# Squeeze-and-excitation gate on one core: keeping 16 rows in PSUM and three more in SBUF between two passes over the input

## Chip, cores and metric

One core of a Trainium2 chip. The time is device microseconds of that core, the median of several executions. "GB/s" is what the core's 16 DMA engines moved.

## The reference, cut to what matters

```python
x: (1, 256, 256, 384) bf16        # 65,536 positions, 384 channels, 50.3 MB
w_down: (384, 24), w_up: (24, 384)

def reference(x, w_down, w_up):
    s = x.mean(axis=(1, 2))
    s = sigmoid(silu(s @ w_down) @ w_up)
    return x * s[:, None, None, :]
```

Every output needs the mean over all positions. So the kernel passes over `x` twice: once to sum it, once to scale it. What is still on the chip after the first pass need not be read again.

## The kernel before

The positions are laid out as 128 partitions of 512 rows; a row is 384 bf16, 768 bytes in each partition, 98,304 bytes in all. Chunks of 16 rows (1.57 MB) go into 17 slots of SBUF. There are 32 chunks: 17 stay in the slots after the first pass ("cached"), 15 do not ("streamed") and are read again.

```python
JS = min(J, max(1, 12288 // (C * 2)))           # 16 rows in a chunk
n_slots = max(1, min(NCH, (avail - small_bytes) // bytes_per_slot))   # 17
NS = NCH - n_slots                               # 15 streamed chunks
p1_order = [(stream_ids[k], k % n_slots) for k in range(NS)] + [
    (cache_ids[i], i) for i in range(n_slots)]
# ... first pass: DMA a chunk (the last one in 8 pieces of 2 rows, the one before in 2),
#     then one matmul with a column of ones per row, all into one PSUM accumulator
nc.sync.dma_start(out=st[:, r0:r0 + rsz, :], in_=x3[:, j0 + r0:j0 + r0 + rsz, :])
nc.tensor.matmul(sums_ps[ci][:1, :csz], ones_bf[:, 0:1], st[:, jj, c0:c0 + csz], start=first, stop=last)
# ... mean, the two small products, sigmoids -> gate [128, 384] bf16
# second pass:
def scale_and_store(sl, ch, piece_rows=None):   # ... cut
    nc.vector.tensor_tensor(out=st[:, r0:r0 + rsz, :], in0=st[:, r0:r0 + rsz, :], in1=gate_b, op=ALU.mult)
    nc.scalar.dma_start(out=out3[:, j0 + r0:j0 + r0 + rsz, :], in_=st[:, r0:r0 + rsz, :])

for i in range(n_slots):        # cached chunks; slot 0 in pieces of 1, 3, 4, 8 rows, slot 1 in 8, 8
    ...
for k in range(NS):             # streamed chunks: read again into slot k, scale, store
    nc.sync.dma_start(out=slots[sl][:, :jsz, :], in_=x3[:, j0:j0 + jsz, :])
    scale_and_store(sl, stream_ids[k])
```

Of the kernel before, what the change touches and what calls it, by code (L numbers as in the profile page):

```python
# [8 lines left out]
ALU = mybir.AluOpType  # L9
ACT = mybir.ActivationFunctionType  # L10
BF16 = mybir.dt.bfloat16
FP32 = mybir.dt.float32


def _pad32(nbytes: int) -> int:
    return ((nbytes + 31) // 32) * 32
# [3 lines left out]
def kernel(  # L20
# [7 lines left out]
    nc = tc.nc  # L28
    P = nc.NUM_PARTITIONS

    B, H, W, C = x.shape
    Cd, R = w_down.shape
# [3 lines left out]
    J = N // P  # L36

    ck_chunks = [(c0, min(128, C - c0)) for c0 in range(0, C, 128)]
    KT = len(ck_chunks)
    cn_chunks = [(c0, min(512, C - c0)) for c0 in range(0, C, 512)]  # L40

    JS = min(J, max(1, 12288 // (C * 2)))
    chunks = [(j0, min(JS, J - j0)) for j0 in range(0, J, JS)]
    NCH = len(chunks)

    bytes_per_slot = _pad32(JS * C * 2)
    small_bytes = (
        _pad32(C * 2)
        + _pad32(8 * 2)
        + _pad32(KT * R * 2)  # L50
        + _pad32(C * 2)
        + _pad32(C * 2)
        + _pad32(KT * 2)
        + _pad32(4)
        + _pad32(P * 2)
        + _pad32(4)
    )
    avail = nc.sbuf_top - nc.sbuf_base
    n_slots = max(1, min(NCH, (avail - small_bytes) // bytes_per_slot))

    NS = NCH - n_slots
    stream_ids = list(range(NS))
    cache_ids = list(range(NS, NCH))

    x3 = x.flatten_outer_dims().rearrange("(p j) c -> p j c", p=P)
    out3 = out.flatten_outer_dims().rearrange("(p j) c -> p j c", p=P)

    slots_pool = ctx.enter_context(tc.tile_pool(name="slots", bufs=1))
    consts = ctx.enter_context(tc.tile_pool(name="consts", bufs=1))
    work = ctx.enter_context(tc.tile_pool(name="work", bufs=1))  # L70
    psum = ctx.enter_context(tc.tile_pool(name="psum", bufs=1, space=bass.MemoryType.PSUM))

    slots = [
        slots_pool.tile([P, JS, C], BF16, name=f"slot{i}") for i in range(n_slots)
    ]

    ones_bf = consts.tile([P, 8], BF16)
# [5 lines left out]
    sums_ps = [  # L83
        psum.tile([1, csz], FP32, name=f"sums_ps_{i}")
        for i, (c0, csz) in enumerate(cn_chunks)
    ]

    p1_order = [(stream_ids[k], k % n_slots) for k in range(NS)] + [
        (cache_ids[i], i) for i in range(n_slots)
    ]  # L90
    total_mm = J
    mm_state = {"idx": 0}

    def read_and_reduce(ch, sl, pieces):
        j0, jsz = chunks[ch]
        st = slots[sl]
        cuts = []
        step = (jsz + pieces - 1) // pieces
        r = 0
        while r < jsz:  # L100
            cuts.append((r, min(step, jsz - r)))
            r += step
        for (r0, rsz) in cuts:
            nc.sync.dma_start(  # L104
                out=st[:, r0:r0 + rsz, :], in_=x3[:, j0 + r0:j0 + r0 + rsz, :]
            )
            for jj in range(r0, r0 + rsz):
                first = mm_state["idx"] == 0
                last = mm_state["idx"] == total_mm - 1
                for ci, (c0, csz) in enumerate(cn_chunks):  # L110
                    nc.tensor.matmul(  # L111
                        sums_ps[ci][:1, :csz],
                        ones_bf[:, 0:1],
                        st[:, jj, c0:c0 + csz],
                        start=first,
                        stop=last,
                    )
                mm_state["idx"] += 1

    for n, (ch, sl) in enumerate(p1_order):  # L120
        remaining = len(p1_order) - n
        if remaining == 1:
            pieces = 8
        elif remaining == 2:
            pieces = 2
        else:
            pieces = 1
        read_and_reduce(ch, sl, pieces)

    wd_sb = consts.tile([P, KT, R], BF16)  # L130
    for kt, (c0, csz) in enumerate(ck_chunks):
        nc.gpsimd.dma_start(out=wd_sb[:csz, kt, :], in_=w_down[c0:c0 + csz, :])  # L132
    wu_sb = consts.tile([R, C], BF16)
    nc.gpsimd.dma_start(out=wu_sb[:R, :], in_=w_up[:, :])  # L134

    mean_bf = work.tile([1, C], BF16)
    for ci, (c0, csz) in enumerate(cn_chunks):
        nc.vector.tensor_scalar(  # L138
            out=mean_bf[:1, c0:c0 + csz],
            in0=sums_ps[ci][:1, :csz],  # L140
            scalar1=1.0 / float(N),
            scalar2=None,
            op0=ALU.mult,
        )

    meanT_ps = psum.tile([P, KT], FP32)
    for kt, (c0, csz) in enumerate(ck_chunks):
        nc.tensor.matmul(  # L148
            meanT_ps[:csz, kt:kt + 1],
            mean_bf[0:1, c0:c0 + csz],  # L150
            ones_bf[0:1, 0:1],
            start=True,
            stop=True,
        )
# [3 lines left out]
    else:  # L158
        for kt, (c0, csz) in enumerate(ck_chunks):
            nc.vector.tensor_copy(  # L160
                out=meanT_sb[:csz, kt:kt + 1], in_=meanT_ps[:csz, kt:kt + 1]
            )

    z1_ps = psum.tile([R, 1], FP32)
    for kt, (c0, csz) in enumerate(ck_chunks):
        nc.tensor.matmul(  # L166
            z1_ps[:R, 0:1],
# [2 lines left out]
            start=(kt == 0),  # L170
            stop=(kt == KT - 1),
# [5 lines left out]
        out=z1bc[:R, :],  # L177
        in0=z1_ps[:R, 0:1].to_broadcast([R, P]),
# [2 lines left out]
        op0=ALU.mult,  # L181
    )

    gate = consts.tile([P, C], BF16)
    for ci, (c0, csz) in enumerate(cn_chunks):
        zz_ps = psum.tile([P, csz], FP32, name=f"zz_ps_{ci}")
        nc.tensor.matmul(  # L187
            zz_ps[:, :csz],
            z1bc[:R, :],
            wu_sb[:R, c0:c0 + csz],  # L190
            start=True,
            stop=True,
        )
        nc.scalar.activation(  # L194
            out=gate[:, c0:c0 + csz], in_=zz_ps[:, :csz], func=ACT.Sigmoid
        )

    def scale_and_store(sl, ch, piece_rows=None):
        j0, jsz = chunks[ch]
        st = slots[sl]  # L200
        if piece_rows is None:
            cuts = [(0, jsz)]
        else:
            cuts = []
            r = 0
            for pr in piece_rows:
                if r >= jsz:
                    break
                pr = min(pr, jsz - r)
                cuts.append((r, pr))  # L210
                r += pr
            if r < jsz:
                cuts.append((r, jsz - r))
        for (r0, rsz) in cuts:
            gate_b = gate[:, None, :].to_broadcast([P, rsz, C])
            nc.vector.tensor_tensor(  # L216
                out=st[:, r0:r0 + rsz, :],
                in0=st[:, r0:r0 + rsz, :],
                in1=gate_b,
                op=ALU.mult,  # L220
            )
            nc.scalar.dma_start(
                out=out3[:, j0 + r0:j0 + r0 + rsz, :], in_=st[:, r0:r0 + rsz, :]
            )

    for i in range(n_slots):
        if i == 0:
            scale_and_store(i, cache_ids[i], piece_rows=[1, 3, 4, 8])
        elif i == 1:
            scale_and_store(i, cache_ids[i], piece_rows=[8, 8])  # L230
        else:
            scale_and_store(i, cache_ids[i])
    for k in range(NS):
        sl = k % n_slots
        j0, jsz = chunks[stream_ids[k]]
        nc.sync.dma_start(out=slots[sl][:, :jsz, :], in_=x3[:, j0:j0 + jsz, :])  # L236
        scale_and_store(sl, stream_ids[k])


# [28 lines left out]
```

## Time and profile before

| | before |
|---|---|
| time, median (12 runs, 306.75 to 307.49) | 307.19 us |
| span of the profiled run | 305.5 us |
| moved by the DMA: read, written | 73.96 MB, 50.33 MB |
| rows read twice | 240 of 512 |
| sum ready, first scale starts | 123.94 us, 126.75 us |
| last scale ends | 253.0 us |

The engines are named as the profiler names them: PE is TensorE, DVE is VectorE, ACT is ScalarE, POOL is GpSimd, SP is SyncE. These lines are from the page of the kernel before: its span, then the busy tenths of DVE and of the DMA engines and the GB/s in 40 equal slices of the span, then two DMA queues (packets, MB, share of the 16 engines) and the HBM total.

```profile
span 305.5 us, 1315 instructions
...
DVE  0000000000000000599999999998444441000000
...
DMA  7999999999999999299999999999999999999996
GB/s 295 420 426 429 423 426 426 425 423 428 425 424 428 425 422 351 74 351 380 436 428 425 434 436 418 434 434 426 426 434 428 428 431 436 425 428 436 426 425 288
...
q1 hardware_dynamic: 7920, 73.93, 57.9%
q10 hardware_dynamic: 5184, 50.33, 39.0%
...
HBM read 73.96 MB, written 50.33 MB: 407 GB/s over the span
```

The DMA engines are 90% or more busy in nearly every slice, and most slices move 418 to 436 GB/s. The hole in slice 17 is the gate: the last input has landed, and nothing can be written yet. DVE is idle for the last six slices, while the DMA works on to the end: the writes have queued up behind it.

The same kernel in chosen stretches. The columns are: stretch, length, busy time (and count) of PE, PE weight loads, DVE, ACT and POOL, then the granted clock, the DMA share and GB/s. A share above 1 comes from counting a packet where it starts.

```profile
core 0: us, PE busy (x) PEld busy (x) DVE busy (x) ACT busy (x) POOL busy (x), PEclk, DMA share, GB/s
24.00:100.00 76.00, 57.44 (x325) 27.44 (x323) 0.00 (x0) 0.00 (x0) 0.00 (x0) 0.98 1.01 425
117.00:121.00 4.00, 4.00 (x27) 2.04 (x25) 0.00 (x0) 0.00 (x0) 0.00 (x0) 1.00 1.05 376
134.00:144.00 10.00, 0.00 (x0) 0.00 (x0) 10.00 (x4) 0.00 (x0) 0.00 (x0) 0.50 1.03 372
150.00:240.00 90.00, 0.00 (x0) 0.00 (x0) 75.53 (x23) 0.00 (x0) 0.00 (x0) 0.50 1.01 430
250.00:295.00 45.00, 0.00 (x0) 0.00 (x0) 2.99 (x1) 0.00 (x0) 0.00 (x0) 0.50 1.01 430
```

Reading alone gets 425 GB/s, mixed reads and writes 430, writes alone 430. So bytes can be turned into time: a row read or not read in the mixed stretch is 98,304 bytes / 430 GB/s = 0.229 us. The Trainium skill, "DMA: Bandwidth & Descriptors" (Where 436 GB/s comes from), puts the ceiling of the SBUF ports at 435 GB/s. This trace stays just under it, at 425 to 430. Two stretches are below that rate. From 117 to 121 us, where the 2-row pieces move (with the end of the two 8-row pieces before them), it is 376. From 134 to 144 us it is 372.

The timeline around the gate (start, length, engine, line, operation, output and inputs, count, and in brackets how long the engine was idle before and for what) and the last scale.

```profile
start us, us, engine line op out<-in xcount [idle before <-releaser]
...
115.48 8.43 PE L111 MATMUL sums_ps<-slot,ones_bf 128*1 128x384 bf16 x48 [0.93 <-DMA slot<-in_x_dram]
...
123.94 0.55 DVE L138 TENSOR_SCALAR mean_bf<-sums_ps 1x384 bf16<-1x384 f32 x1 [123.07 <-PE sums_ps L111]
...
126.75 1.90 DVE L216 TENSOR_TENSOR slot<-slot,gate 128x384 bf16<-128x384 bf16 x3 [0.95 <-ACT gate L194]
```

```profile
249.63 3.36 DVE L216 TENSOR_TENSOR slot<-slot,gate 128x6144 bf16<-128x6144 bf16 x1 [3.98 <-DMA slot<-in_x_dram]
```

The last full chunk lands at about 115.5 us; PE then does the 48 rows that are left in one go, 8.4 us, and DVE turns the sum into the mean at 123.94. The first scale starts at 126.75. The last scale ends at 249.63 + 3.36 = 253.0 us, 50 us before the last write lands.

### The profile page before, as it was taken

What the parts mean: (1) busy time and instruction counts of PE and PEld (TensorE: products, weight loads), DVE (VectorE), ACT (ScalarE), POOL (GpSimd) and SP (SyncE); (2) the same over time, 40 slices, a digit from 0 to 9 for tenths busy, and PEclk for the clock granted to TensorE, in tenths of its full rate; (3) what the DMA queues carried; (4) which work ended last, traced back from release to release, by engine and by line L of the source; (5) the groups of instructions that cost most, each with busy time, mean ns of one, the idle gap of its engine ahead of it and who ended that gap; (6) DMA issues with size and microseconds to landing.
All of it is one profiled execution on the core that took longest, in us unless ns stands there. A gap on an engine that the chain in (4) does not pass through costs nothing.

```text
span 305.5 us, 1315 instructions
## 1 busy us (share of the span) xinstructions
PE 92.7 (30%) x519; PEld 44.3 (14%) x519; DVE 106.6 (35%) x40; ACT 2.1 (1%) x4; POOL 2.5 (1%) x8
## 2 busy tenths in 40 slices
PE   0977787777777778300000000000000000000000
PEld 0433333333333334100000000000000000000000
DVE  0000000000000000599999999998444441000000
ACT  1000000000000000000000000000000000000000
POOL 3000000000000000000000000000000000000000
PEclk9999899999999999855555555555555555555555
DMA  7999999999999999299999999999999999999996
GB/s 295 420 426 429 423 426 426 425 423 428 425 424 428 425 422 351 74 351 380 436 428 425 434 436 418 434 434 426 426 434 428 428 431 436 425 428 436 426 425 288
DMA packets 13238, 124.38 MB, mean 407 GB/s; under 512 B 1572, under 2 KB 2736, under 8 KB 3632
## 3 DMA queue, kind: packets, MB, share of 16 engines
q1 hardware_dynamic: 7920, 73.93, 57.9%
q10 hardware_dynamic: 5184, 50.33, 39.0%
q8 instruction: 4, 0.07, 0.1%
q0 software_dynamic: 128, 0.04, 0.1%
q14 instruction: 2, 0.02, 0.0%
HBM read 73.96 MB, written 50.33 MB: 407 GB/s over the span
## 4 chain that ended last, share of the span: by engine, by line
DMA 57%; DVE 21%; PE 3%; SPq 1%; issue 0%; ACT 0%
DMA slot<-in_x_dram 45%; DVE slot L216 20%; DMA out_dram<-slot 12%; PE sums_ps L111 3%; SPq L104 1%; DVE mean_bf L138 0%; ACT gate L194 0%; DVE z1bc L176 0%; PE zz_ps L187 0%; PE meanT_ps L148 0%; PE z_ps L166 0%; DVE meanT_sb L157 0%; ACT s L174 0%; SPq L236 0%
## 5 line engine op out<-in xcount | busy, mean ns | idle before, releaser
L216 DVE TENSOR_TENSOR slot<-slot,gate 128x6144 bf16<-128x6144 bf16 (+4 forms) x36 | 105.5, 2995 | 21.7 <-DMA slot<-in_x_dram 20.7
L111 PE MATMUL sums_ps<-slot,ones_bf 128*1 128x384 bf16 x512 | 91.9, 335 | 32.0 <-DMA slot<-in_x_dram 32.0
L111 PEld LDWEIGHTS <-ones_bf 128*1 128x1 bf16 x512 | 43.8, 86 | 79.7 <-issue 42.8
L138 DVE TENSOR_SCALAR mean_bf<-sums_ps 1x384 bf16<-1x384 f32 x1 | 0.5, 545 | 123.1 <-PE sums_ps L111 123.1
L132 POOL DMA_DIRECT2D wd_sb<-in_w_down_dram x3 | 1.8, 605 | 0.8 <-POOLq L252 0.8
L81 ACT ACT_TABLE_LOAD x1 | 1.3, 1283 | 0.7 <-PEq L252 0.7
L174 ACT ACTIVATE s<-z_ps 24x1 f32<-24x1 f32 x1 | 0.2, 160 | 123.0 <-PE z_ps L166 123.0
L134 POOL DMA_DIRECT2D wu_sb<-in_w_up_dram x1 | 0.5, 539 | 0.0
L187 PE MATMUL zz_ps<-wu_sb,z1bc 24*128 24x384 bf16 x1 | 0.3, 331 | 0.6 <-DVE z1bc L176 0.6
L176 DVE TENSOR_SCALAR z1bc<-z_ps,s 24x128 bf16<-24x128 f32 x1 | 0.3, 339 | 0.5 <-ACT s L174 0.5
L194 ACT ACTIVATE gate<-zz_ps 128x384 bf16<-128x384 f32 x1 | 0.5, 491 | 0.8 <-PE zz_ps L187 0.8
L148 PE MATMUL meanT_ps<-ones_bf,mean_bf 1*128 1x1 bf16 x3 | 0.2, 163 | 0.6 <-DVE mean_bf L138 0.6
L78 DVE MEMSET ones_bf<- 128x8 bf16 x1 | 0.1, 65 | 0.8 <-PEq L252 0.8
L166 PE MATMUL z_ps<-meanT_sb,wd_sb 128*24 128x1 bf16 x3 | 0.2, 163 | 0.3 <-DVE meanT_sb L157 0.3
L148 PEld LDWEIGHTS <-mean_bf 1*128 1x128 bf16 x3 | 0.1, 92 | 1.0 <-DVE mean_bf L138 1.0
L157 DVE CAST meanT_sb<-meanT_ps 128x3 bf16<-128x3 f32 x1 | 0.2, 165 | 0.3 <-PE meanT_ps L148 0.3
L166 PEld LDWEIGHTS <-wd_sb 128*24 128x24 bf16 x3 | 0.2, 90 | 0.3 <-issue 0.2
L81 ACT ACTIVATE dummy<-ones_bf 1x1 f32<-1x1 bf16 x1 | 0.2, 202 | 0.0
L187 PEld LDWEIGHTS <-z1bc 24*128 24x128 bf16 x1 | 0.1, 90 | 0.7 <-DVE z1bc L176 0.7
L252 POOL MEMSET const-bfloat16-1.0<- 128x1 bf16 x1 | 0.1, 102 | 0.0
L252 POOL MEMSET const-float32-0.0<- 128x1 f32 x1 | 0.1, 100 | 0.2 <-issue 0.2
L252 POOL MEMSET const-float32-1.0<- 128x1 f32 x1 | 0.1, 100 | 0.0
(1 smaller groups left out, 0.1 us busy)
## 6 DMA issues: line engine op xcount, KB each, us to landing
slot<-in_x_dram SPq DMA_DIRECT2D x45, 1536.0 KB, 29.4
out_dram<-slot ACTq DMA_DIRECT2D x30, 1536.0 KB, 29.2
out_dram<-slot ACTq DMA_DIRECT2D x3, 768.0 KB, 3.7
slot<-in_x_dram SPq DMA_DIRECT2D x2, 768.0 KB, 26.8
slot<-in_x_dram SPq DMA_DIRECT2D x8, 192.0 KB, 11.7
out_dram<-slot ACTq DMA_DIRECT2D x1, 384.0 KB, 2.4
out_dram<-slot ACTq DMA_DIRECT2D x1, 288.0 KB, 2.1
out_dram<-slot ACTq DMA_DIRECT2D x1, 96.0 KB, 1.7
```

What stands on the lines that cost most here:

```text
L81: nc.scalar.activation(out=dummy[:1, :1], in_=ones_bf[0:1, 0:1], func=ACT.Sigmoid)
L104: nc.sync.dma_start(out=st[:, r0:r0 + rsz, :], in_=x3[:, j0 + r0:j0 + r0 + rsz, :])
L111: nc.tensor.matmul(sums_ps[ci][:1, :csz], ones_bf[:, 0:1], st[:, jj, c0:c0 + csz], start=first, stop=last,)
L132: nc.gpsimd.dma_start(out=wd_sb[:csz, kt, :], in_=w_down[c0:c0 + csz, :])
L134: nc.gpsimd.dma_start(out=wu_sb[:R, :], in_=w_up[:, :])
L138: nc.vector.tensor_scalar(out=mean_bf[:1, c0:c0 + csz], in0=sums_ps[ci][:1, :csz], scalar1=1.0 / float(N), scalar2=None, op0=ALU.mult,)
L148: nc.tensor.matmul(meanT_ps[:csz, kt:kt + 1], mean_bf[0:1, c0:c0 + csz], ones_bf[0:1, 0:1], start=True, stop=True,)
L166: nc.tensor.matmul(z1_ps[:R, 0:1], wd_sb[:csz, kt, :], meanT_sb[:csz, kt:kt + 1], start=(kt == 0), stop=(kt == KT - 1),)
L187: nc.tensor.matmul(zz_ps[:, :csz], z1bc[:R, :], wu_sb[:R, c0:c0 + csz], start=True, stop=True,)
L194: nc.scalar.activation(out=gate[:, c0:c0 + csz], in_=zz_ps[:, :csz], func=ACT.Sigmoid)
L216: nc.vector.tensor_tensor(out=st[:, r0:r0 + rsz, :], in0=st[:, r0:r0 + rsz, :], in1=gate_b, op=ALU.mult,)
L252: nc = _bacc.Bacc("TRN2", target_bir_lowering=False, num_devices=1)
```

## The change

Intent: read fewer rows twice. PSUM has room that the kernel does not use. The new kernel copies the first chunk into six PSUM banks (parts of PSUM; one holds 1,024 bf16 in each partition) during the first pass and scales it from there at the very end. It also saves small tiles: `mean` and `gate` are laid over `w_up`'s tile. With that the last slot holds 19 rows instead of 16. Rows read twice: 512 - 16 (PSUM) - (17 x 16 + 3) (slots) = 221 instead of 240. They are one chunk of 13 rows, now first in order, and 13 chunks of 16.

The Trainium skill, "PSUM — Partial Sum Buffer" (Specifications (TRN2)), lists no DMA access to PSUM, and for VectorE only writes of 4-byte types. That is why the rows go through a slot and DVE on the way in and on the way out, and why the copy in is done on pairs of bf16 seen as fp32.

The diff, cut to its core:

```diff
+    n_slots = max(1, min((J + JS - 1) // JS, (avail - bytes_small) // slot_bytes))      # 17
+    spare = avail - bytes_small - n_slots * slot_bytes
+    extra_rows = max(0, min(spare // _pad32(C * 2), max(0, J - n_slots * JS)))          # 3
+    PR = JS  # rows kept in PSUM
+    streamed_rows = J - cached_rows - PR
+    rem = streamed_rows % JS
+    if rem:
+        stream_chunks.append((j0, rem))        # 13 rows, first
+        j0 += rem
 ...
+    pbanks = [psum.tile([P, 512], FP32, name=f"pbank{b}") for b in range(NB)]           # 6
+    misc_ps = psum.tile([P, 512], FP32, name="misc_ps")      # all small results of the gate
 ...
+    LAST = [6, 5, 4, 2, 2]                     # pieces of the last slot; before: 8 of 2 rows
+    read_and_reduce(0, PR, 14)                 # first chunk, through slot 14
+    flat0 = slots[14].rearrange("p r c -> p (r c)")
+    for b in range(NB):
+        nc.vector.tensor_copy(out=pbanks[b][:, :],
+            in_=flat0[:, b * 1024:(b + 1) * 1024].bitcast(FP32))
 ...
-    gate = consts.tile([P, C], BF16)
+    gate = wu_mean                             # w_up, the mean and the gate share a tile
 ...  (after the last streamed chunk)
+    e = 0
+    while e < PR * C:                          # 14 pieces: whole rows, and parts of rows
+        ...                                    #   where a bank ends inside a row
+        nc.vector.tensor_tensor(out=dst, in0=src, in1=g, op=ALU.mult)     # PSUM -> slot 14
+        e += n
+    nc.scalar.dma_start(out=out3[:, 0:PR, :], in_=slots[14][:, :PR, :])
```

More of the change, by code (lines that the diff above doesn't have):

```diff
@@ L42 @@
     JS = min(J, max(1, 12288 // (C * 2)))
-    chunks = [(j0, min(JS, J - j0)) for j0 in range(0, J, JS)]
-    NCH = len(chunks)
-    bytes_per_slot = _pad32(JS * C * 2)
-    small_bytes = (
-        _pad32(C * 2)
-        + _pad32(8 * 2)
+    MP = 32 if R <= 32 else 0
+    bytes_small = (
+        _pad32(8 * 2)
         + _pad32(KT * R * 2)
         + _pad32(C * 2)
-        + _pad32(C * 2)
+        + (_pad32(C * 2) if MP == 0 else 0)
         + _pad32(KT * 2)
@@ L58 @@
     avail = nc.sbuf_top - nc.sbuf_base
-    n_slots = max(1, min(NCH, (avail - small_bytes) // bytes_per_slot))
-    NS = NCH - n_slots
-    stream_ids = list(range(NS))
-    cache_ids = list(range(NS, NCH))
+    slot_bytes = _pad32(JS * C * 2)
+    n_slots = max(1, min((J + JS - 1) // JS, (avail - bytes_small) // slot_bytes))
+    spare = avail - bytes_small - n_slots * slot_bytes
+    extra_rows = max(0, min(spare // _pad32(C * 2), max(0, J - n_slots * JS)))
+    slot_rows = [JS] * n_slots
+    slot_rows[-1] = JS + extra_rows if J > n_slots * JS else min(JS, J - (n_slots - 1) * JS)
+    cached_rows = min(J, sum(slot_rows))
+    PR = JS
+    streamed_rows = J - cached_rows - PR
+    stream_chunks = []
+    j0 = PR
+    rem = streamed_rows % JS
+    if rem:
+        stream_chunks.append((j0, rem))
+        j0 += rem
+    while j0 < PR + streamed_rows:
+        stream_chunks.append((j0, JS))
+        j0 += JS
+    NS = len(stream_chunks)
+    cache_chunks = []
+    j0 = PR + streamed_rows
+    for i in range(n_slots):
+        rows = min(slot_rows[i], J - j0)
+        if rows <= 0:
+            break
+        cache_chunks.append((j0, rows))
+        j0 += rows
+    assert j0 == J
+    n_slots = len(cache_chunks)
     x3 = x.flatten_outer_dims().rearrange("(p j) c -> p j c", p=P)
@@ L73 @@
     slots = [
-        slots_pool.tile([P, JS, C], BF16, name=f"slot{i}") for i in range(n_slots)
+        slots_pool.tile([P, slot_rows[i], C], BF16, name=f"slot{i}")
+        for i in range(n_slots)
     ]
@@ L86, with reduce_rows, read_and_reduce @@
     ]
-    p1_order = [(stream_ids[k], k % n_slots) for k in range(NS)] + [
-        (cache_ids[i], i) for i in range(n_slots)
-    ]
+    NB = PR * C // 1024
+    pbanks = [psum.tile([P, 512], FP32, name=f"pbank{b}") for b in range(NB)]
+    misc_ps = psum.tile([P, 512], FP32, name="misc_ps")
     total_mm = J
     mm_state = {"idx": 0}
-    def read_and_reduce(ch, sl, pieces):
-        j0, jsz = chunks[ch]
+    def reduce_rows(st, r0, rsz):
+        for jj in range(r0, r0 + rsz):
+            first = mm_state["idx"] == 0
+            last = mm_state["idx"] == total_mm - 1
+            for ci, (c0, csz) in enumerate(cn_chunks):
+                nc.tensor.matmul(
+                    sums_ps[ci][:1, :csz],
+                    ones_bf[:, 0:1],
+                    st[:, jj, c0:c0 + csz],
+                    start=first,
+                    stop=last,
+                )
+            mm_state["idx"] += 1
+    def read_and_reduce(j0, jsz, sl, pieces=1):
         st = slots[sl]
@@ L99, in read_and_reduce @@
         r = 0
-        while r < jsz:
-            cuts.append((r, min(step, jsz - r)))
-            r += step
+        for n in LAST if pieces == 4 else [step] * pieces:
+            cuts.append((r, n))
+            r += n
+        assert r == jsz
         for (r0, rsz) in cuts:
@@ L106, in read_and_reduce @@
             )
-            for jj in range(r0, r0 + rsz):
-                first = mm_state["idx"] == 0
-                last = mm_state["idx"] == total_mm - 1
-                for ci, (c0, csz) in enumerate(cn_chunks):
-                    nc.tensor.matmul(
-                        sums_ps[ci][:1, :csz],
-                        ones_bf[:, 0:1],
-                        st[:, jj, c0:c0 + csz],
-                        start=first,
-                        stop=last,
-                    )
-                mm_state["idx"] += 1
-    for n, (ch, sl) in enumerate(p1_order):
-        remaining = len(p1_order) - n
+            reduce_rows(st, r0, rsz)
+    LAST = [6, 5, 4, 2, 2]
+    read_and_reduce(0, PR, 14)
+    flat0 = slots[14].rearrange("p r c -> p (r c)")
+    for b in range(NB):
+        nc.vector.tensor_copy(
+            out=pbanks[b][:, :],
+            in_=flat0[:, b * 1024:(b + 1) * 1024].bitcast(FP32),
+        )
+    for k, (j0, jsz) in enumerate(stream_chunks):
+        read_and_reduce(j0, jsz, k)
+    for i, (j0, jsz) in enumerate(cache_chunks):
+        remaining = n_slots - i
         if remaining == 1:
-            pieces = 8
+            pieces = 4
         elif remaining == 2:
@@ L127 @@
             pieces = 1
-        read_and_reduce(ch, sl, pieces)
+        read_and_reduce(j0, jsz, i, pieces=pieces if jsz >= pieces else 1)
     wd_sb = consts.tile([P, KT, R], BF16)
@@ L132 @@
         nc.gpsimd.dma_start(out=wd_sb[:csz, kt, :], in_=w_down[c0:c0 + csz, :])
-    wu_sb = consts.tile([R, C], BF16)
-    nc.gpsimd.dma_start(out=wu_sb[:R, :], in_=w_up[:, :])
-    mean_bf = work.tile([1, C], BF16)
+    wu_mean = consts.tile([P, C], BF16)
+    nc.gpsimd.dma_start(out=wu_mean[:R, :], in_=w_up[:, :])
+    if MP == 0:
+        mean_t = work.tile([1, C], BF16, name="mean_bf")
+        mean_row = mean_t[0:1, :]
+        ones_row = ones_bf[0:1, 0:1]
+    else:
+        mean_row = wu_mean[MP:MP + 1, :]
+        ones_row = ones_bf[MP:MP + 1, 0:1]
     for ci, (c0, csz) in enumerate(cn_chunks):
         nc.vector.tensor_scalar(
-            out=mean_bf[:1, c0:c0 + csz],
+            out=mean_row[:, c0:c0 + csz],
             in0=sums_ps[ci][:1, :csz],
@@ L144 @@
         )
-    meanT_ps = psum.tile([P, KT], FP32)
+    meanT_ps = misc_ps[:, 384:384 + KT]
     for kt, (c0, csz) in enumerate(ck_chunks):
@@ L149 @@
             meanT_ps[:csz, kt:kt + 1],
-            mean_bf[0:1, c0:c0 + csz],
-            ones_bf[0:1, 0:1],
+            mean_row[:, c0:c0 + csz],
+            ones_row,
             start=True,
@@ L162 @@
             )
-    z1_ps = psum.tile([R, 1], FP32)
+    z1_ps = misc_ps[:R, 400:401]
     for kt, (c0, csz) in enumerate(ck_chunks):
@@ L182 @@
     )
-    gate = consts.tile([P, C], BF16)
+    gate = wu_mean
     for ci, (c0, csz) in enumerate(cn_chunks):
-        zz_ps = psum.tile([P, csz], FP32, name=f"zz_ps_{ci}")
+        zz_ps = misc_ps[:, 0:csz]
         nc.tensor.matmul(
@@ L189 @@
             z1bc[:R, :],
-            wu_sb[:R, c0:c0 + csz],
+            wu_mean[:R, c0:c0 + csz],
             start=True,
@@ L196, with scale_and_store @@
         )
-    def scale_and_store(sl, ch, piece_rows=None):
-        j0, jsz = chunks[ch]
-        st = slots[sl]
+    def scale_and_store(st, j0, jsz, piece_rows=None):
         if piece_rows is None:
@@ L224, in scale_and_store @@
             )
-    for i in range(n_slots):
+    for i, (j0, jsz) in enumerate(cache_chunks):
+        st = slots[i]
         if i == 0:
-            scale_and_store(i, cache_ids[i], piece_rows=[1, 3, 4, 8])
+            scale_and_store(st, j0, jsz, piece_rows=[1, 3, 4, 8])
         elif i == 1:
-            scale_and_store(i, cache_ids[i], piece_rows=[8, 8])
+            scale_and_store(st, j0, jsz, piece_rows=[8, 8])
         else:
-            scale_and_store(i, cache_ids[i])
-    for k in range(NS):
-        sl = k % n_slots
-        j0, jsz = chunks[stream_ids[k]]
-        nc.sync.dma_start(out=slots[sl][:, :jsz, :], in_=x3[:, j0:j0 + jsz, :])
-        scale_and_store(sl, stream_ids[k])
+            scale_and_store(st, j0, jsz)
+    for k, (j0, jsz) in enumerate(stream_chunks):
+        st = slots[k]
+        nc.sync.dma_start(out=st[:, :jsz, :], in_=x3[:, j0:j0 + jsz, :])
+        scale_and_store(st, j0, jsz)
+    e = 0
+    while e < PR * C:
+        b, o = divmod(e, 1024)
+        pb = pbanks[b][:, :].bitcast(BF16)
+        c = e % C
+        n = min(C - c, 1024 - o)
+        if c == 0 and n == C:
+            k = (1024 - o) // C
+            n = k * C
+            src = pb[:, o:o + n].rearrange("p (k c) -> p k c", c=C)
+            dst = slots[14][:, e // C:e // C + k, :]
+            g = gate[:, None, :].to_broadcast([P, k, C])
+        else:
+            src, dst, g = pb[:, o:o + n], flat0[:, e:e + n], gate[:, c:c + n]
+        nc.vector.tensor_tensor(out=dst, in0=src, in1=g, op=ALU.mult)
+        e += n
+    nc.scalar.dma_start(out=out3[:, 0:PR, :], in_=slots[14][:, :PR, :])
 _INS = ['x', 'w_down', 'w_up']
```

## The prediction

> **What bounds the kernel now.** The DMA. The page's slices show the 16 DMA engines 90% or more busy in nearly all of 40 slices; the table of stretches gives 425 GB/s for 24 to 100 us (reads for the sum), 430 for 150 to 250 (reads and writes mixed), 429 for 256 to 300 (writes only). The page's queue list has 124.38 MB: 32 chunks read once (50.3 MB), 15 of them read again (23.6 MB), 32 written (50.3 MB). One row of 128x384 bf16 is 98,304 bytes, 0.229 us at 429 GB/s. Not bandwidth: the start (PE first runs at 7.1 us), and about 122 to 127.5 us, where the gate is made and no DMA moves, with a ramp of writes after it.
>
> DVE is not the limit: its last scale ends at 253.0 us (timeline), and for 50 us after that only queued writes drain. PE needs 0.163 us per row (16 rows in 2.76 us), less than the DMA.
>
> **What the change does.** It keeps 16 rows per partition in six PSUM banks, and uses spare SBUF (gained partly by laying mean and gate over w_up) to make the last slot 19 rows (its pieces 6+5+4+2+2 fix that). Rows read twice fall from 240 to 512-16-(17x16+3) = 221: 19 rows, 1.87 MB. They leave the second phase, which is saturated: 19 x 0.229 = 4.35 us, all on the critical path.
>
> The last slot is read in five pieces in place of eight of 2 rows. The table of stretches shows 367 to 384 GB/s while the 2-row pieces (1,536 bytes a partition) move, 117 to 121 us. At 372 GB/s, 1.57 MB costs 0.55 us more than at 427. Four such rows are left of sixteen: about 0.4 us gained. PE works off a backlog there (48 matmuls in 8.4 us), with three more rows after the last full chunk (0.5 us), which lands 0.7 us earlier. I take 0.4 us.
>
> **Added work.** Six DVE copies to PSUM at about 7 us, when DVE is idle: free. At the end DVE scales the PSUM rows in 14 pieces. The Trainium skill, "VectorE: DVE Perf Modes" (The perf-mode tier table), says tensor_tensor with a PSUM operand runs at 1x, where bf16 in SBUF gets 2x. This trace shows 3.26 to 3.36 us per 16 rows from SBUF; twice that plus piece overheads is an estimate of 7 to 9 us. It starts at about 245 us, and slot 14's earlier write (landed at 234.7 in the chain of waits) is done by then. The last write is issued only at about 271 us. So it is hidden. The gate stage may change by 0.1 us.
>
> **Sum.** 307.37 - 4.35 - 0.4 = 302.6 us (ratio 0.985). Range 301.7 to 303.9. Chances: faster by over 2% 0.05, within 2% 0.94, slower 0.01.
>
> **What would show it right.** Queue list: 122.5 MB in all; the rate in the mixed stretch still about 430 GB/s. First scale after the gate at about 126.3 us instead of 126.75. DVE's PSUM scales end more than 20 us before the end of the span.
>
> **What would make it wrong.** If DVE's PSUM part waits for slot 14's write, or takes so long that the last write starts with an empty queue (up to +5 us); if the sharing of tiles adds waits to the gate stage; if the PSUM copies delay slot 14's reuse; if the 13-row chunk shifts the order of reads and writes and changes the second phase's rate.

## The result, and the profile after

| | before | after |
|---|---|---|
| time, median | 307.19 us (12 runs) | 302.14 us (8 runs, 301.93 to 302.32) |
| ratio | | 0.9836, 95% interval 0.9826 to 0.9846 |
| span of the profiled run | 305.5 us | 300.3 us |
| read by the DMA | 73.96 MB | 72.09 MB |
| first scale starts | 126.75 us | 126.62 us |
| last scale ends | 253.0 us | 248.8 us |

A ratio is the mean time of one kernel's runs over that of the other's of the same rounds, so it is not quite the ratio of the medians quoted. Executions over 1.5% slower than the fastest of the same kernel are left out of the means. The result is correct against the reference. The gain is 5.05 us; the prediction said 4.75, counted from 307.37 us, the median of the first four runs of the kernel before.

The page of the changed kernel, the same lines as before:

```profile
span 300.3 us, 1332 instructions
...
DVE  0400000000000000299999999999644481000000
...
DMA  7999999999999999189999999999999999999996
GB/s 289 426 422 426 427 424 426 431 419 424 429 428 422 426 427 403 69 327 393 419 424 440 419 444 421 430 432 421 444 421 437 435 415 437 421 442 422 434 429 296
...
q1 hardware_dynamic: 7344, 72.06, 57.2%
q10 hardware_dynamic: 5184, 50.33, 39.7%
...
HBM read 72.09 MB, written 50.33 MB: 408 GB/s over the span
```

Reads are down by 1.87 MB and writes are as they were. DVE's busy digit in the second slice is the copy into PSUM.

The same stretches of the changed kernel:

```profile
core 0: us, PE busy (x) PEld busy (x) DVE busy (x) ACT busy (x) POOL busy (x), PEclk, DMA share, GB/s
24.00:100.00 76.00, 55.28 (x321) 26.74 (x320) 0.00 (x0) 0.00 (x0) 0.00 (x0) 1.00 1.01 426
117.00:121.00 4.00, 4.00 (x27) 2.05 (x25) 0.00 (x0) 0.00 (x0) 0.00 (x0) 1.00 1.01 394
134.00:144.00 10.00, 0.00 (x0) 0.00 (x0) 10.00 (x4) 0.00 (x0) 0.00 (x0) 0.50 1.02 396
150.00:240.00 90.00, 0.00 (x0) 0.00 (x0) 75.40 (x23) 0.00 (x0) 0.00 (x0) 0.50 1.01 429
250.00:295.00 45.00, 0.00 (x0) 0.00 (x0) 0.00 (x0) 0.00 (x0) 0.00 (x0) 0.50 1.01 432
```

The saturated stretches are unchanged: 426, 429, 432 GB/s. The stretch of small pieces improved from 376 to 394. The stretch from 134 to 144 us went from 372 to 396, which nothing in the prediction accounts for.

The timeline around the gate, and at the end:

```profile
114.95 8.82 PE L124 MATMUL sums_ps<-slot,ones_bf 128*1 128x384 bf16 x51 [0.93 <-DMA slot<-in_x_dram]
...
123.81 0.55 DVE L182 TENSOR_SCALAR wu_mean<-sums_ps 1x384 bf16<-1x384 f32 x1 [112.94 <-PE sums_ps L124]
...
126.62 1.89 DVE L258 TENSOR_TENSOR slot<-slot,wu_mean 128x384 bf16<-128x384 bf16 x3 [0.95 <-ACT wu_mean L238]
```

```profile
241.36 3.36 DVE L258 TENSOR_TENSOR slot<-slot,wu_mean 128x6144 bf16<-128x6144 bf16 x1 [4.05 <-DMA slot<-in_x_dram]
244.63 4.19 DVE L294 TENSOR_TENSOR slot<-pbank,wu_mean 128x768 bf16<-128x768 bf16 x14
270.18 0.34 ACTq L296 DMA_DIRECT2D out_dram<-slot  x1
```

The sum is ready at 123.81 instead of 123.94, and the first scale starts 0.13 us earlier, not the 0.4 that was predicted. PE has 51 rows to do once the last full chunk has landed and takes 8.82 us for them. At the end DVE goes from the last streamed chunk to the PSUM rows without a wait, ends at 244.63 + 4.19 = 248.8 us, and the write of those rows is not issued until 270.18. ACT issues the earlier writes before it, and they are far behind (a full one takes 29.2 us from issue to landing). The span ends at 300.3.

DVE's groups by shape, the kernel before first (line, engine, operation, tiles, shapes, count, busy us, mean ns of one, idle time before):

```profile
line engine op names shapes xcount | busy us, mean ns | idle before us <-releasers
L216 DVE TENSOR_TENSOR slot<-slot,gate 128x6144 bf16<-128x6144 bf16 x30 | 98.7, 3350 | 20.7 <-DMA slot<-in_x_dram 20.7
L216 DVE TENSOR_TENSOR slot<-slot,gate 128x3072 bf16<-128x3072 bf16 x3 | 5.1, 1750 | 0.0
```

```profile
L258 DVE TENSOR_TENSOR slot<-slot,wu_mean 128x6144 bf16<-128x6144 bf16 x27 | 88.9, 3350 | 16.0 <-DMA slot<-in_x_dram 15.9
...
L152 DVE COPY pbank<-slot 128x512 f32<-128x512 f32 x6 | 3.7, 685 | 6.3 <-DMA slot<-in_x_dram 6.3
L294 DVE TENSOR_TENSOR slot<-pbank,wu_mean 128x768 bf16<-128x768 bf16 x6 | 3.2, 545 | 0.0
...
L294 DVE TENSOR_TENSOR slot<-pbank,wu_mean 128x256 bf16<-128x256 bf16 x4 | 1.1, 278 | 0.0
...
L294 DVE TENSOR_TENSOR slot<-pbank,wu_mean 128x128 bf16<-128x128 bf16 x4 | 0.8, 212 | 0.0
```

From SBUF, 3,072 elements more cost 3350 - 1750 = 1600 ns, 0.52 ns each. From PSUM, 768 - 256 = 512 elements more cost 545 - 278 = 267 ns, also 0.52 ns each. The scale out of PSUM runs at the same rate for each element as that out of SBUF. The prediction had taken twice the time per element from the Trainium skill and expected 7 to 9 us; 4.19 were measured. The copies into PSUM take 685 ns each at about 7 us, when DVE has nothing else to do.

Where the 5.05 us went, by sums: 19 rows x 0.229 us = 4.35; the start of the second pass 0.13 earlier; and the stretch from 134 to 144 us, 24 GB/s more for 10 us = 0.24 MB, at 430 GB/s 0.56 us. Together 5.04. This adds up, but it is arithmetic on two traces, and a start 0.13 us earlier is within the scatter: in the changed kernel and in the two with a repeated scale below, which are the same up to there, the first scale starts at 126.62, 126.78 and 126.53 us. The experiments take it apart.

### The profile page after: what moved, and what is told of

The parts are those of the page before. It is cut to its first block, busy times and chain, and to the rows that moved or that the text cites. A ratio compares the mean times of both kernels' runs of the same rounds, so it can differ in the third digit from the quotient of the medians.

```text
span 300.3 us, 1332 instructions
## 1 busy us (share of the span) xinstructions
PE 90.9 (30%) x519; PEld 43.8 (15%) x519; DVE 111.0 (37%) x59; ACT 2.1 (1%) x4; POOL 2.5 (1%) x8
## 2 busy tenths in 40 slices
DMA packets 12663, 122.52 MB, mean 408 GB/s; under 512 B 1508, under 2 KB 1904, under 8 KB 3184
## 3 DMA queue, kind: packets, MB, share of 16 engines
HBM read 72.09 MB, written 50.33 MB: 408 GB/s over the span
## 4 chain that ended last, share of the span: by engine, by line
DMA 71%; DVE 6%; issue 3%; PE 1%; ACT 0%; DVEq 0%; SPq 0%; ACTq 0%
DMA slot<-in_x_dram 45%; DMA out_dram<-slot 26%; DVE slot L258 5%; DVE slot L294 1%; PE sums_ps L124 1%; DVE wu_mean L182 0%; ACT wu_mean L238 0%; DVEq L322 0%; SPq L143 0%; DVE z1bc L220 0%; PE misc_ps L231 0%; PE misc_ps L192 0%; PE misc_ps L210 0%; DVE meanT_sb L201 0%; ACT s L218 0%
## 5 line engine op out<-in xcount | busy, mean ns | idle before, releaser
L258 DVE TENSOR_TENSOR slot<-slot,wu_mean 128x6144 bf16<-128x6144 bf16 (+6 forms) x35 | 102.1, 2984 | 16.9 <-DMA slot<-in_x_dram 15.9
L124 PE MATMUL sums_ps<-slot,ones_bf 128*1 128x384 bf16 x512 | 90.2, 331 | 33.6 <-DMA slot<-in_x_dram 33.5
L152 DVE COPY pbank<-slot 128x512 f32<-128x512 f32 x6 | 3.7, 685 | 6.3 <-DMA slot<-in_x_dram 6.3
L294 DVE TENSOR_TENSOR slot<-pbank,wu_mean 128x768 bf16<-128x768 bf16 (+2 forms) x14 | 4.2, 374 | 0.0
## 6 DMA issues: line engine op xcount, KB each, us to landing
out_dram<-slot ACTq DMA_DIRECT2D x28, 1536.0 KB, 29.2
```

Source lines behind the costliest of these rows:

```text
L152: nc.vector.tensor_copy(out=pbanks[b][:, :], in_=flat0[:, b * 1024:(b + 1) * 1024].bitcast(FP32),)
L294: nc.vector.tensor_tensor(out=dst, in0=src, in1=g, op=ALU.mult)
```

## The experiments

The theory: the time follows the rows read twice, at 0.229 us each, since the second pass is bound by the DMA throughout; all the rest is small. Rivals: that the gain comes from the pieces of the last slot, or from the order of the re-reads (a short chunk first), and that the scale out of PSUM is not hidden.

All experiments were correct against the reference. "Before" of the same rounds was 307.23 us (the first four below), 307.25 (the repeated scale, the first timing of the seven banks, and the seven banks with finer writes) and 307.19 (the last four to be run: the second timing of the seven banks, finer writes with six, and the two short first re-reads).

### The PSUM rows alone

```diff
-    extra_rows = max(0, min(spare // _pad32(C * 2), max(0, J - n_slots * JS)))
+    extra_rows = 0
-    LAST = [6, 5, 4, 2, 2]
+    LAST = [4, 4, 4, 2, 2]
```

> The 16 rows in PSUM alone; the last slot keeps 16 rows (read as 4+4+4+2+2) and all 14 streamed chunks have 16 rows, 224 rows read twice. If the time follows the rows read twice (0.229 us each), it is 16 x 0.229 = 3.67 us below the kernel before, 303.5 us, plus at most 0.1 to 0.2 less for the pieces. If the extra gain of the changed kernel (0.7 us over the rows' 4.35) came with the PSUM part or the gate's new layout, it is about 302.8.

Measured: 303.17 us (303.00 to 303.56, 4 runs), ratio 0.9867 [0.9852, 0.9882]. That is 4.06 us less, where 16 rows and the pieces make 3.8. The interval (0.46 us to either side) holds the difference, so whether 0.26 us more came with PSUM or the gate's layout can't be told; the full 0.7 us more (302.8) did not come.

### The three extra rows alone

```diff
-    PR = JS  # rows kept in PSUM
+    PR = 0  # no rows kept in PSUM
-    read_and_reduce(0, PR, 14)
-    nc.scalar.dma_start(out=out3[:, 0:PR, :], in_=slots[14][:, :PR, :])
```

> The three extra rows in the last slot alone, nothing in PSUM: 237 rows read twice, and the first chunk read again has 13 rows in place of 16. By rows alone 3 x 0.229 = 0.69 us less than before, 306.5 us. If the short first chunk also removes the dip of the DMA rate at 140 to 142 us that only the kernel before has (0.7 us by the table of stretches), it is 305.8.

Measured: 306.14 us (306.01 to 306.26, 5 runs), ratio 0.9965 [0.9952, 0.9977]: 1.09 us less, between the two expectations. The two parts add up: 4.06 + 1.09 = 5.15 us against 5.05 for both (each of them also has the larger pieces, so that small part is counted twice). Sixteen rows in PSUM are worth four fifths of the change, three rows in SBUF a fifth. Per row the three bring more than the sixteen; the reason is under "The short chunk last instead of first".

### The pieces alone

```diff
     def read_and_reduce(ch, sl, pieces):
+        sizes = [5, 4, 3, 2, 2] if pieces == 8 else None
...
-            cuts.append((r, min(step, jsz - r)))
-            r += step
+            n = sizes[len(cuts)] if sizes else min(step, jsz - r)
+            cuts.append((r, n))
+            r += n
```

> The kernel before with the last slot read as 5+4+3+2+2 rows in place of eight times 2. My prediction's term says 0.4 us less (306.8). The changed kernel's trace shows the first scale only 0.13 us earlier, so the rival says 0.1 to 0.15 us less, hardly to be told from none (307.0).

Measured: 307.10 us (306.90 to 307.32, 5 runs), ratio 0.9997 [0.9985, 1.001]. No difference can be told. Its timeline:

```profile
115.71 8.10 PE L113 MATMUL sums_ps<-slot,ones_bf 128*1 128x384 bf16 x48 [0.95 <-DMA slot<-in_x_dram]
...
123.84 0.55 DVE L140 TENSOR_SCALAR mean_bf<-sums_ps 1x384 bf16<-1x384 f32 x1 [122.97 <-PE sums_ps L113]
```

The larger pieces do move faster, 391 GB/s from 117 to 121 us against 376, but far from the 427 that the prediction took, and the sum ends only 0.10 us earlier. The packet records say why: the last packet of the first pass ends at 122.79 us here and at 122.88 in the kernel before, and in all 14 traces the sum is ready 1.00 to 1.11 us after that packet. In the ten kernels with 6+5+4+2+2 rows it ends at 122.57 to 122.88 us, so the reads themselves end 0 to 0.3 us earlier and not 0.4.

PE also leaves little room: one row after the other costs it about 0.163 us (16 rows take 2.76 us, of which the last 0.16 is one matmul's own tail), so the 48 rows after the last full chunk need at least 48 x 0.163 + 0.16 = 8.0 us, and 8.10 were measured. In the kernel before, where PE also waited for the small pieces, it was 8.43. That 0.33 us less became only 0.10 because the last full chunk happened to land 0.23 us later in this trace, though the instructions up to there are the same: one trace of each can't settle a tenth.

### The short chunk last instead of first

```diff
-    if rem:
-        stream_chunks.append((j0, rem))
-        j0 += rem
-    while j0 < PR + streamed_rows:
+    while j0 + JS <= PR + streamed_rows:
         stream_chunks.append((j0, JS))
         j0 += JS
+    if rem:
+        stream_chunks.append((j0, rem))
+        j0 += rem
```

> The changed kernel with the 13-row chunk as the last of the streamed chunks in place of the first, all else equal, 221 rows read twice. If the part of the gain beyond the rows (0.7 us) comes from the short first re-read, it is 302.8 us and the DMA rate dips between 134 and 146 us as it does in the kernel before. If it has another source, it stays at 302.1.

Measured: 302.45 us (302.36 to 302.50, 4 runs), ratio 0.9845 [0.9832, 0.9858], about 0.3 us more than the changed kernel. The ratios' intervals overlap, so the time alone does not settle it, but the traces do. The lines for 134 to 144 us of this kernel, of the extra rows alone, and of the PSUM rows alone:

```profile
134.00:144.00 10.00, 0.00 (x0) 0.00 (x0) 10.00 (x4) 0.00 (x0) 0.00 (x0) 0.50 1.02 367
```

```profile
134.00:144.00 10.00, 0.00 (x0) 0.00 (x0) 10.00 (x4) 0.00 (x0) 0.00 (x0) 0.50 1.02 393
```

```profile
134.00:144.00 10.00, 0.00 (x0) 0.00 (x0) 10.00 (x4) 0.00 (x0) 0.00 (x0) 0.50 1.01 368
```

GB/s are 367, 393, 368. The two kernels whose first re-read has 13 rows reach 393 and 396; the four whose first re-read has 16 rows (before, pieces alone, PSUM alone, short chunk last) have 367 to 372. So the dip follows the order of the re-reads, not PSUM, and not the number of rows read twice. This is also why the three extra rows brought more than 3 x 0.229: that kernel's first re-read is the short one.

A fixed stretch is a rough measure when transfers shift. Counted instead over the first 24 us after the first write packet, as time lost against a steady 430 GB/s (worked out from all packets' sizes and times), the four kernels with 16 rows first lose 3.0 to 3.2 us, and the four with 13 rows and the same first writes (after, extra rows alone, the two repeated scales below) 2.6. So the short chunk first is worth about 0.5 us there. These first 24 us or so are called the ramp below.

The packet records of the traces also show where the dip sits. For the first re-read, in ns per KB of 1,000 bytes (mean of 16 packets at a time, in order of start; the time is that since the first write packet of the output), worked out from the packets' sizes and durations:

```
                       about 8 us ............................ about 13 us
before (16 rows)       37.4 37.4 37.8 39.7 46.7 59.6 53.8 61.7
short_last (16 rows)   39.6 37.4 38.0 38.2 45.0 55.6 56.0 63.0
after (13 rows)        37.6 38.4 37.6 37.6 37.6 38.8 43.5 57.1   (ends at about 12 us)
```

With 16 rows packets are slow from about 11 us after the first write on, with 13 rows from 11.6 to 12; the shorter read has less left by then. In the steady part of the second pass nearly all packets take 37.4.

### The scale out of PSUM, eight and sixteen times

```diff
-        nc.vector.tensor_tensor(out=dst, in0=src, in1=g, op=ALU.mult)
+        for _ in range(8):      # and 16
+            nc.vector.tensor_tensor(out=dst, in0=src, in1=g, op=ALU.mult)
```

> The changed kernel with each of the 14 scales out of PSUM done eight times (same result). In the trace of the changed kernel they take 4.19 us once and end at 248.8 us; eight times is 33.5 us, to about 278 us, 8 us after the last write was issued (270.2) but before the queue of writes runs dry. If the PSUM scale is hidden behind the queued writes, the time stays at 302.1 to 302.4. If it is exposed, as a rival to my prediction has it, it is up to 29 us more.

> The same sixteen times: 67 us, ending at about 311.7 us, after the 15 other streamed and cached writes have drained (about 295 us). The last write of 1.57 MB then takes some 5.6 us alone, so the span is about 317.3 us against 300.3 and the time about 319 us. This tells how much slack the PSUM scale has: about 45 us, if scale_x8 does not show and this one costs 17.

Measured: 302.40 us (302.32 to 302.59, 4 runs) and 318.24 us (317.93 to 318.39, 4 runs). The timelines of the two at the end:

```profile
core 0 of [0], span 300.8 us
...
244.78 33.05 DVE L295 TENSOR_TENSOR slot<-pbank,wu_mean 128x768 bf16<-128x768 bf16 x112
277.86 0.34 ACTq L297 DMA_DIRECT2D out_dram<-slot  x1
```

```profile
core 0 of [0], span 316.2 us
...
244.22 65.88 DVE L295 TENSOR_TENSOR slot<-pbank,wu_mean 128x768 bf16<-128x768 bf16 x224
310.14 0.34 ACTq L297 DMA_DIRECT2D out_dram<-slot  x1
```

Eight times as much work (33.05 us) delays the last write's issue from 270.18 to 277.86 us and costs 0.3 us by the medians (302.40 against 302.14), which the intervals do not tell from nothing. Sixteen times (65.88 us, to 310.1) leaves the DMA without work (0 GB/s from 300 to 310 us), and the last write ends the span 6.1 us later at 316.2 (the 5.6 us expected for it was an estimate given without its working). So by estimate DVE could have ended at about 300.3 - 6.1 = 294 us without a loss, 45 us later than it does. Whether the scale takes 4.19 us or the 7 to 9 us of the prediction does not matter to the time.

### The seventh bank

The sum and the gate's small results share one bank, so seven hold rows: 18 of them, 219 rows read twice, and 11 in the first re-read.

```diff
-    PR = JS  # rows kept in PSUM
+    PR = 18  # rows kept in PSUM
-    sums_ps = [psum.tile([1, csz], FP32, name=f"sums_ps_{i}") for ...]
+    misc_ps = psum.tile([P, 512], FP32, name="misc_ps")
+    sums_ps = [misc_ps[:, 0:C]]
-    read_and_reduce(0, PR, 14)            # and slot 14 -> slot 16 wherever the PSUM rows pass; cuts for the part-filled bank left out
+    read_and_reduce(0, PR, 16)
```

> The changed kernel with the sum and the gate's small results in one bank, so that seven banks hold 18 rows: 219 rows read twice, two fewer. By rows 2 x 0.229 = 0.46 us less than the changed kernel; the first re-read has 11 rows in place of 13, which may save another 0.1 to 0.3 us in the ramp. 301.4 to 301.7. If rows no longer count, 302.1.

Measured the first time: 302.6 to 307.3 us (6 runs), median 303.53, ratio 0.9891 [0.9851, 0.9931] without the slowest run. That is useless for half a microsecond, so the same kernel was run again:

> The seven banks again, the same kernel, for its first timing was spread from 302.6 to 307.3 us. If the chip was disturbed then, it is 301.5 to 301.8 with a spread of some 0.3 us. If the kernel itself is unsteady, the spread of 1 us or more comes again.

Measured: 301.74 us (301.60 to 302.62, 4 runs), ratio 0.9828 [0.9815, 0.984]. This is what the rows promise (302.14 - 0.46 = 301.7), with one run of four still 0.9 us higher. That the 11-row first re-read would save more in the ramp is not seen: in the trace of the second timing none of its packets is slow, but write packets after it are (45 to 53 ns per KB at 15 to 17 us), and the ramp loses 2.65 us, as with 13 rows. What disturbed the first set is open. Its kept profile, of a run of 303.7 us, has no worse a ramp; the loss is later (425 GB/s from 150 to 200 us, against 429 in the second timing). The runs of the kernel before in the same rounds were steady (306.97 to 307.59).

### Finer first writes

```diff
-            scale_and_store(st, j0, jsz, piece_rows=[1, 3, 4, 8])    # slot 0
+            scale_and_store(st, j0, jsz, piece_rows=[1, 3, 4, 4, 4])
-            scale_and_store(st, j0, jsz, piece_rows=[8, 8])          # slot 1
+            scale_and_store(st, j0, jsz, piece_rows=[4, 4, 8])
```

With seven banks:

> The last one with the first writes cut finer, 1, 3, 4, 4, 4 rows of the first slot and 4, 4, 8 of the second, in place of 1, 3, 4, 8 and 8, 8. All traces show half a microsecond without any transfer at 130.5 us, when the 4-row write is done and the 8-row one not yet scaled. By the hole 0.4 to 0.5 us less than the seven banks with the coarse cuts. If the smaller writes cost as much as the hole, no difference.

Measured: 301.40 us (301.35 to 301.90, 5 runs), ratio 0.9817 [0.9804, 0.9829]. That is 0.3 us less than the second timing of the seven banks; the intervals overlap, so the gain is not told from none.

With six:

> The changed kernel with six banks, and the first writes cut 1, 3, 4, 4, 4 and 4, 4, 8. If the two rows in the seventh bank gave what they should (0.46 us) in the kernel with both, this is 301.4 + 0.5 = 301.9, that is hardly below the changed kernel. If the finer cuts gave that gain, it is 301.4 to 301.6.

Measured: 302.76 us (302.60 to 302.78, 4 runs), ratio 0.9854 [0.9841, 0.9867]: 0.6 us slower than the changed kernel, a miss of both expectations (the intervals overlap a little, the runs do not). The stretch of 134 to 144 us, six banks first:

```profile
134.00:144.00 10.00, 0.00 (x0) 0.00 (x0) 10.00 (x4) 0.00 (x0) 0.00 (x0) 0.50 1.01 345
```

```profile
134.00:144.00 10.00, 0.00 (x0) 0.00 (x0) 10.00 (x4) 0.00 (x0) 0.00 (x0) 0.50 0.99 391
```

The half microsecond without transfers at 130.5 us is gone in both. In the six-bank kernel the loss came back, with more, in the stretch after it: 345 GB/s against 396. In the seven-bank kernel it is 391. The packets show what moved: with the finer writes the first re-read starts 6.8 us (six banks) and 5.7 us (seven) after the first write instead of 8.0, and its packets are slow at once, 39 to 96 and 39 to 62 ns per KB (means of 16). With six banks no write packet starts from 7 to 10 us, so there the reads are slow on their own. The ramp loses 3.2 us with six banks and 2.5 with seven. A ramp is not improved by closing one hole in it, if what follows starts at another moment.

### A short first re-read, with nothing else changed

```diff
-    chunks = [(j0, min(JS, J - j0)) for j0 in range(0, J, JS)]
+    chunks = [(0, 8), (8, 8)] + [(j0, JS) for j0 in range(JS, J, JS)]
```

> The kernel before with its first chunk of 16 rows cut into two chunks of 8 in two slots, so that the first read of the second phase is 8 rows long; 240 rows are read twice as before. In the six kernels with a 16-row or a 13-row first re-read, its packets are slow only from about 11 us after the first write on; an 8-row read ends by about then. If the short first re-read alone gives the gain beyond the rows, this is 0.4 to 0.6 us below the kernel before (306.7) and the first-re-read packets all run at 38 to 40 ns per KB. If the gain came otherwise, 307.2.

Measured: 307.89 us (307.13 to 308.59, 6 runs), ratio 1.0023 [1.0008, 1.0037]. Not faster, rather slower and less steady. The packets show that nothing was gained in the ramp. An 8-row read into the first slot only has to wait for the first 8 rows of that slot to be written, so it starts 5.3 us after the first write, not 8.0. Its packets are slow from the start (99 ns per KB in the first 16, down to 38 in the last), though no write packet starts from 6 to 7 us. The ramp loses 3.1 us, as in the kernel before; the stretch of 134 to 144 us, at 390 GB/s, would not tell. Why the kernel is also slower later on is open. So "a short first re-read is good" is not the cause in general. What the runs show is narrower: with the re-read starting at the same 8.0 us, 13 rows lose less than 16.

### Seven banks with a short first re-read

Finer cuts in slot 0 only; the 11 odd rows are read again as 8 and 3 in two slots. The edits for seven banks are left out of this cut.

```diff
-    if rem:
-        stream_chunks.append((j0, rem))
-        j0 += rem
+    for n in (8, rem - 8):
+        stream_chunks.append((j0, n))
+        j0 += n
-            scale_and_store(st, j0, jsz, piece_rows=[1, 3, 4, 8])
+            scale_and_store(st, j0, jsz, piece_rows=[1, 3, 4, 4, 4])
```

> Seven banks, fine cuts in the first slot only (1, 3, 4, 4, 4 and 8, 8), and the 11 odd rows read again as 8 and 3 rows in two slots, so that the first re-read is 8 rows. If short first re-reads avoid the slow packets, this loses 0.5 us less in the ramp than the seven banks with fine cuts: about 301.0. If not, 301.4.

Measured: 301.67 us (301.65 to 301.68, 5 runs), ratio 0.9819 [0.9807, 0.9832]: no gain over the seven banks with fine cuts (301.40). Its first re-read, too, starts early (4.7 us) and slow (77 ns per KB in the first 16 packets). But so does that of the seven banks with fine cuts, and the ramp loses 2.4 us here and 2.5 there, so an early start alone does not decide.

The best kernel is the seven banks with fine cuts, 301.40 us, 0.6 to 0.7 us below the changed kernel; the intervals of their ratios just overlap (0.9804 to 0.9829 and 0.9826 to 0.9846).

## Why the prediction was right

- **The bound.** Right. The saturated stretches run at 429 to 432 GB/s before and after, and fewer bytes gave less time.
- **The rows, 4.35 us.** Right in size: PSUM alone and extra rows alone gave 4.06 and 1.09 us for 3.67 and 0.69, the excess of the first lies within its interval, and that of the second is of the size of what the shorter first re-read saves in the ramp (0.5 us). The bytes came out as said (122.52 MB in all).
- **The pieces, 0.4 us.** Too large. Alone they gave 0.13 us that cannot be told from nothing, and the first scale came at 126.62 us, not 126.3. The term that was off is the rate: the prediction let twelve of sixteen rows go from 372 to 427 GB/s, but with the larger pieces the stretch moved 391 to 394, and the last read packet ended 0.09 us (pieces alone) and 0.18 us (changed kernel) earlier. The prediction itself had noted PE's backlog, and then took the DMA's gain in full. The three rows more of the last slot cost PE about what the earlier landing gave (114.95 instead of 115.48 us, 51 rows instead of 48).
- **What was not in it.** The ramp of the second pass moves 396 instead of 372 GB/s from 134 to 144 us, 0.56 us by the profile and 0.5 by the count from the first write. Putting the short chunk last takes the rate back to 367, and about 0.3 us of time. The prediction had named the order of reads as a possible loss; it was a gain. The two errors of size partly cancel: 0.3 too much, about 0.5 missing, so 4.75 predicted and 5.05 measured. That the total came so near is in part luck.
- **The scale out of PSUM.** Right that it is hidden, with a margin larger than said: 51 us before the end, 45 us of slack by the repeated scale. The estimate of 7 to 9 us was wrong; it took 4.19.
- **Tile sharing in the gate.** No wait was added: from the mean to the first scale it is 2.81 us in both (123.94 to 126.75, 123.81 to 126.62).

Open: why packets of the first re-read are slow from 11 or 12 us after the first write, and for early re-reads at once, even where no writes run beside them; why the kernel with the 8-row first re-read is slower after the ramp; and what disturbed the first timing of the seven banks.

## What to carry to other kernels

In a kernel that reads its input twice and keeps the DMA saturated, any memory that can hold a row is worth that row's transfer time, PSUM included, as long as the copy in falls into idle DVE time and the copy out is placed where the write queue is already far behind. Before crediting larger transfers with the full rate, look at what the last packet and the engine behind it do: here the reads ended 0.1 to 0.2 us earlier instead of 0.4, and PE's own rows after the last full chunk left little more to gain. The first ten to fifteen microseconds of a phase that mixes reads and writes can move by half a microsecond either way with the size and the start of single transfers, so changes there have to be measured one by one.

## What the Trainium skill lacked or had wrong

- "VectorE: DVE Perf Modes", The perf-mode tier table, gives tensor_tensor with any PSUM operand 1x. Here tensor_tensor with one bf16 operand in PSUM, the other and the output in SBUF, took 545, 278 and 212 ns for 768, 256 and 128 elements, 0.52 ns for each one more, the same as from SBUF (0.52 ns by 3350 and 1750 ns for 6,144 and 3,072). The same page's section Why PSUM operands drop a tier, which leaves the 2x mode for 16-bit types open, fits the measurement; the table does not.
- "DMA: Bandwidth & Descriptors", Where 436 GB/s comes from, says that for transfers between HBM and SBUF the HBM side, about 358 GB/s, binds. With this one core running, the traces show 425 for reads, 430 for reads and writes mixed and 430 for writes. The sentence does not say that it is meant for two cores that share the HBM; the same page's section Measured does, and its figure for one core is 425 too.
- No page tells of slow reads in the first microseconds after writes have begun: 45 to 64 ns per KB in the later half of a 16-row first re-read, and up to 99 for one started earlier (in one kernel 49 to 96 while no write packet started), against 37.4 in the steady state.
